# One list for the order of all operations and their engines, in an attention and MoE kernel

## The chip, the cores and the metric

The kernel runs on one core of one Trainium2 chip. The metric is the device time of one launch in microseconds, the median over repeated runs. A core has five instruction queues that the kernel writes: TensorE (PE in the profile, with its weight loads as PEld), VectorE (DVE), ScalarE (ACT), GpSimd (POOL) and SyncE (SP), which issues almost all DMAs. Each queue runs its instructions strictly in the order in which the program gives them; a semaphore makes one wait for another.

## The reference

```python
q_bits = einsum(q, proj) > 0;  k_bits = einsum(k, proj) > 0     # 6 bits: a bucket of each query and key
mask = q_bucket[..., :, None] == k_bucket[..., None, :]
scores = where(mask, q @ k.T / sqrt(64), -1e9)
attn = exp(scores - max); attn = attn / (sum(attn) + 1e-9)
x = (attn @ v), heads side by side                                # 4 batches, 8 heads, 768 x 64 -> 3072 x 512
out = ((x @ w_a) * (x @ w_b)) @ w_out                             # 512 -> 1536 -> 512
```

q, k, v and proj come as float32. The three weight matrices come as float64, 18.9 MB together, and are made into 32-bit floats on the chip.

## The kernel before, in words

**Tiling.** The 3072 tokens are cut into 14 chunks, `CHUNKS`: the first four hold 128 tokens of batch 0, the other ten 256 tokens. Attention is done in units of one head and 128 queries (`qtile`): scores of 128 queries against 768 keys (L1215, with the mask folded in as 12 more rows of the product), the row maximum (L1235, tile `mx`), its scale and bias (`affine`, L1243 and L1247), the exponential (L1256, tile `e`), a turn of the result, and the product with v. The eight units of chunk 0 are turned on TensorE in 32 bits (`turned`, tiles `et` and `at`, copied out by L639); all later ones are split into two 16-bit halves (`by_dma`: a cast by L639 and a subtraction by L642, tile `a`) and turned by a DMA. `su_end` divides by the sum (tile `x`, L1335) and turns x to `xT`. `moe` multiplies a chunk by the weights: first products `ab` (L1442 in 32 bits for chunks 0 and 1, L1450 in 16 bits for the rest), their elementwise product `g` (L1471, L1479), and second products `o` (L1515).

**The start.** k, q and v of batch 0 are loaded in head pairs. `split` scales each into a high and a low half: a gram product on TensorE (L675) bounds the magnitude, VectorE reads it (L662) and makes a power of two (`powers`, L625 and L628); then come the high half (`high`, tile `kt` or `qt`), the low half (L748), turns by TensorE and their copies (L639, tiles `trk`, `trq`), and the bits. v is bounded likewise, and `parts` makes its halves `vh` and `vl` (L1051). The weights come in 18 pieces of two loads each (`to_f32`): ScalarE and one of ScalarE and GpSimd work on the raw words (L955; L945 or L947), and VectorE merges them (L963, tile `wz`). Only three staging slots exist, so a load waits until the merge of three pieces earlier is done, and all that stands behind it on SyncE waits too. Each group of weights has a gram product as well (L981). Beside chunks 0 and 1 the weights are split into 16-bit halves (`halved`, L906).

**What sets the order.** Nothing is issued where it is written. The body only calls `op(engine, duration, function, key, reads, writes, ...)`, which records 3727 operations with their dependencies; `Plan.issue` then issues them. In the kernel before it runs a small event model of the engines, with durations written beside each operation: whenever an engine is free, the ready operation with the lowest number in `PLACES` (one number for each operation, lines 62 to 255) goes next. Where an operation could run on several engines, `ENGINES` gives the one, or the engine that is free first takes it. The model holds VectorE back while GpSimd is busy (`PORT_WAIT`) for operations marked `sbuf`, and counts buffers so that no tile is asked for before one is free. The order in which the model issues is the order of the queues on the chip; the model's times go nowhere else.

The small projection is loaded in two pieces through ScalarE's queue, though the model counts them on SyncE (L579). Two operations, for the identity in 16 bits, issue nothing (one ahead of L586, one in `bounds`); the copy itself stands inside another operation (L740, L861).

Of the kernel before, what the change touches and what calls it, by code (L numbers as in the profile page):

```python
# [61 lines left out]
PLACES = (  # L62
# [234 lines left out]
    3481: "DVE", 3489: "DVE", 3497: "DVE", 3505: "ACT", 3514: "ACT", 3522: "DVE", 3538: "DVE", 3547: "DVE",  # L297
    3568: "ACT", 3576: "ACT", 3584: "ACT", 3592: "DVE", 3601: "ACT", 3634: "DVE", 3635: "DVE", 3725: "DVE",
}

def free(b, **durs):
# [27 lines left out]
HOP = 0.2  # L331
# [35 lines left out]
class Plan:  # L367
# [32 lines left out]
    def issue(self):  # L400
# [4 lines left out]
        for o in ops:  # L405
            o.succs, o.npred, o.ready = [], len(o.preds), 0.0
# [1212 lines left out]
```

## Time and profile before

| what | before |
|---|---|
| median of 3 runs | 903.46 us (902.1 to 903.72) |
| profiled execution, first to last instruction | 900.4 us |
| median less that span | 3.06 us |
| TensorE busy | 871.8 us, 97% |
| VectorE, ScalarE, GpSimd busy | 624.4, 573.4, 450.9 us |
| DMA | 145.31 MB, mean 161 GB/s |

The page of the profile gives only the span for the profiled execution, so its own time is the span and the 3.06 us by which the median is longer. TensorE is busy for nearly the whole span; where it is not, and where it runs at a lower clock, is told by the views by stretch of time.

### The profile page before, as it was taken

The numbers are of one execution on the slowest core, as the hardware profiler recorded it, in microseconds if no ns is written. First come the engines' busy times: TensorE is split into PE (matmuls) and PEld (weight loads), VectorE is DVE, ScalarE is ACT, GpSimd is POOL, SyncE is SP. The second block draws the span as 40 slices with busy tenths as digits, with TensorE's granted clock in tenths as the row PEclk, the third lists the DMA queues.
The fourth block names the chain that finished last, engine by engine and source line by source line (L and its number), as shares of the span: only waits on it lengthen the run. The fifth ranks groups of instructions, "written<-read, shape, count | busy, mean of one in ns | idle before, by whom it ended". The sixth has DMA issues, their size and how long they took to land.

```text
span 900.4 us, 24310 instructions
## 1 busy us (share of the span) xinstructions
PE 871.8 (97%) x9761; PEld 673.8 (75%) x9761; DVE 624.4 (69%) x1446; ACT 573.4 (64%) x1125; POOL 450.9 (50%) x377
## 2 busy tenths in 40 slices
PE   5798999999999999999999999999999999999998
PEld 4677788786877777777777777777777777777775
DVE  6889878897778666777776686777778576633211
ACT  5986565677776878666766675667676466654222
POOL 1255456555735665554455556635556457544111
PEclk9699999999999999999999999999999999999999
DMA  9898667599998999998976788698986757755100
GB/s 331 262 319 232 124 112 158 124 179 220 190 230 148 170 163 161 177 209 169 176 161 128 149 175 169 115 214 170 179 183 148 124 136 130 147 95 100 32 24 24
DMA packets 430433, 145.31 MB, mean 161 GB/s; under 512 B 404080, under 2 KB 422640, under 8 KB 430320
## 3 DMA queue, kind: packets, MB, share of 16 engines
q1 hardware_dynamic: 430160, 143.76, 76.8%
q8 instruction: 76, 1.25, 0.6%
q14 instruction: 37, 0.30, 0.1%
q10 hardware_dynamic: 160, 0.00, 0.0%
HBM read 37.82 MB, written 6.29 MB: 49 GB/s over the span
## 4 chain that ended last, share of the span: by engine, by line
PE 85%; DVE 9%; DMA 2%; issue 2%; ACT 1%; POOL 0%; SPq 0%; DVEq 0%; ACTq 0%; POOLq 0%
PE ab L1450 37%; PE o L1515 20%; PE s L1215 12%; PE av L1284 10%; PE ab L1442 4%; DVE mx L1235 2%; DVE wz L963 1%; PE kt L766 1%; DMA wz<-in_moe_w_out_dram 1%; DVE wz L906 1%; DMA wz<-in_moe_w_b_dram 1%; DMA wz<-in_moe_w_a_dram 1%; DMA pj<-in_proj_dram 0%; PE qb L787 0%; DVE g L1479 0%
## 5 line engine op out<-in xcount | busy, mean ns | idle before, releaser
L642 POOL TENSOR_TENSOR a<-e,a 128x768 f16<-128x768 f32 x184 | 309.4, 1686 | 199.3 <-DVE a L639 87.9
L1450 PE MATMUL ab<-xT,wz 128*128 128x256 f16 (+1 forms) x3456 | 377.5, 264 | 1.4 <-DVE g L1479 1.0
L1450 PEld LDWEIGHTS <-wz 128*128 128x128 f16 x3456 | 310.9, 98 | 52.5 <-issue 3.5
L1256 ACT ACTIVATE e<-s,bias,sc 128x768 f32<-128x768 f32 x192 | 189.8, 989 | 107.4 <-DVE bias L1247 84.5
L1235 DVE TENSOR_REDUCE mx<-s 128x1 f32<-128x768 f32 x192 | 182.7, 953 | 64.1 <-PE s L1215 59.0
L1515 PE MATMUL o<-wz,g 128*128 128x512 f16 (+1 forms) x840 | 215.6, 392 | 0.1
L1495 POOL TENSOR_TENSOR g<-g,g 128x256 f16<-128x256 f32 x132 | 95.8, 726 | 170.8 <-ACT g L1490 164.3
L1215 PE MATMUL s<-trk,trq 76*128 76x384 f16 (+1 forms) x768 | 157.6, 330 | 3.8 <-ACT e L1256 2.5
L1479 DVE SCALAR_TENSOR_TENSOR g<-ab,ab,a 128x256 f32<-128x256 f32 x132 | 63.4, 480 | 105.6 <-ACT a L1471 88.0
L1284 PEld LDWEIGHTS <-at 128*128 128x128 f16 x3312 | 116.9, 98 | 16.2 <-issue 1.7
L1515 PEld LDWEIGHTS <-g 128*128 128x128 f16 x792 | 73.8, 98 | 68.8
L1471 ACT ACTIVATE a<-ab,ab 128x256 f32<-128x256 f32 x132 | 62.2, 471 | 96.2 <-PE ab L1450 79.8
L1284 PE MATMUL av<-vh,at 128*128 128x64 f16 x2208 | 121.6, 193 | 0.7 <-DMA at<-a 0.7
L1215 PEld LDWEIGHTS <-trq 76*128 76x128 f16 (+1 forms) x768 | 70.7, 99 | 45.7 <-issue 9.5
L639 ACT CAST a<-e 128x768 f16<-128x768 f32 x105 | 87.0, 829 | 3.4 <-DMA at<-a 1.4
L1490 ACT CAST g<-g 128x256 f16<-128x256 f32 x132 | 53.0, 401 | 51.3 <-DVE g L1479 41.1
L1284 PE MATMUL av<-vl,at 128*128 128x64 f16 x1104 | 62.3, 193 | 0.0
L639 DVE CAST a<-e 128x768 f16<-128x768 f32 x71 | 42.2, 596 | 14.6 <-ACT e L1256 13.7
L1442 PE MATMUL ab<-xT,wz 128*128 128x128 f32 x384 | 48.1, 278 | 1.3 <-DVE xT L639 0.8
L1442 PEld LDWEIGHTS ab<-xT,wz 128*128 128x128 f32 x384 | 45.5, 192 | 4.6 <-DVE xT L639 1.5
L1247 DVE TENSOR_SCALAR bias<-mx,sc 128x1 f32<-128x1 f32 x180 | 38.6, 214 | 6.3
L1243 DVE TENSOR_SCALAR sc<-mx,cq 128x1 f32<-128x1 f32 x180 | 38.1, 212 | 4.8
(170 smaller groups left out, 775.4 us busy)
## 6 DMA issues: line engine op xcount, KB each, us to landing
rk<-in_k_dram SPq DMA_DIRECT2D x16, 384.0 KB, 4.2
rq<-in_q_dram SPq DMA_DIRECT2D x24, 256.0 KB, 3.5
wz<-in_moe_w_a_dram SPq DMA_DIRECT2D x12, 512.0 KB, 5.7
wz<-in_moe_w_b_dram SPq DMA_DIRECT2D x12, 512.0 KB, 5.3
wz<-in_moe_w_out_dram SPq DMA_DIRECT2D x12, 512.0 KB, 5.7
out_dram<-osb SPq DMA_DIRECT2D x24, 256.0 KB, 2.5
vr<-in_v_dram SPq DMA_DIRECT2D x12, 384.0 KB, 4.7
at<-a SPq DMA_TRANSPOSE x184, 3.5
```

Of the source, the lines that this page charges most:

```text
L639: {"ACT": nc.scalar.copy, "DVE": nc.vector.tensor_copy, "POOL": nc.gpsimd.tensor_copy}[e](out=out, in_=x)
L642: (nc.gpsimd if e == "POOL" else nc.vector).tensor_tensor(out=out, in0=x, in1=y, op=ALU.subtract)
L1215: nc.tensor.matmul(ps.t[:, jj, :HALF], lhsT=trq.t[rows, i, (2 * j + h) * nt + t], rhs=tr.t[rows, i, k0 : k0 + NT // 2].rearrange("p n s -> ...
L1235: lambda: nc.vector.tensor_reduce(out=mx.t[:, col], in_=halves(ps.t), axis=AX.XY, op=ALU.max, negate=True),
L1256: lambda: nc.scalar.activation(flat2(e.t), halves(ps.t), AF.Exp, bias=bias.t[:, col], scale=sc.t[:, col], accum_out=sm.t[:, u : u + 1],),
L1284: nc.tensor.matmul(av.t[:, u, :], lhsT=at.t[:, a + kt, :], rhs=w.t[:, h, kt, :], start=i == 0, stop=i == 3 * NT - 1,)
L1442: nc.tensor.matmul(pl.t[:, m, to], lhsT=wt32(m, cc, f), rhs=xt.t[:, cc * nt // NC, cc * nt % NC : cc * nt % NC + nt, :], start=cc == 0, st ...
L1450: nc.tensor.matmul(pl.t[:, m, to], lhsT=wt(m, wi, cc, f), rhs=xt.t[:, cc * nt // NC, xi, cc * nt % NC : cc * nt % NC + nt, :], start=i == ...
L1471: lambda a=a, pl=pl, gr=gr, sc_of=sc_of: nc.scalar.activation(a.t, pl.t[:, 0, :CH], AF.Copy, scale=sc_of(gr)),
L1479: lambda a=a, g32=g32, pl=pl, gr=gr, sc_of=sc_of: nc.vector.scalar_tensor_tensor(out=g32.t, in0=pl.t[:, 1, :CH], scalar=sc_of(gr + 1), in1 ...
L1495: lambda g=g, g32=g32, g_of=g_of: nc.gpsimd.tensor_tensor(out=g_of(g[1]), in0=g32.t, in1=g_of(g[0]), op=ALU.subtract),
L1515: nc.tensor.matmul(po[u].t.rearrange("p a b -> p (a b)"), lhsT=x()[:, us], rhs=w, start=f == 0 and i == 0, stop=f == NF - 1 and i == len(t ...
```

## The change

`PLACES`, `ENGINES` and the event model in `Plan.issue` go. In their place stand `ORDER`, one list of the 3725 operations that are left, and `ENGINE_OF`, the engine of each operation that has a choice. `issue` walks through the list, asserts that every operation comes after those it depends on and that buffers suffice, and issues it. The two operations that issue nothing go, and what they stood for is stated as reads and writes of the operations that copy the identity. The two loads of the projection are counted on ScalarE's queue, through which they went already. No instruction is added or taken away.

```diff
-PLACES = (
-    372, 36, 26, 591, 571, 25, 386, 254, 1614, 66, 385, 210, 155, 399, 576, 261, 194, 687, 615, 294, 3076, 750, 536,
...
+ORDER = (
+    2, 1, 75, 11, 76, 4, 3, 77, 5, 78, 79, 80, 81, 0, 12, 13, 14, 15, 6, 282, 281, 9, 10, 84, 27, 16, 82, 17, 83, 18,
...
-ENGINES = {
-    17: "DVE", 20: "ACT", 27: "ACT", 33: "DVE", 36: "DVE", 43: "ACT", 49: "DVE", 52: "DVE", 53: "ACT DVE",
...
+ENGINE_OF = {
+    "ACT": (
+        19, 20, 35, 36, 42, 58, 64, 67, 74, 83, 84, 90, 105, 107, 119, 128, 138, 140, 149, 157, 159, 166, 168, 176, 178,
...
     def issue(self):
-        ops = self.ops
-        for o, place in zip(ops, PLACES):
-            o.key = place
-            o.eng = ENGINES.get(o.seq, o.eng)
...
+        engine = {n: e for e, ns in ENGINE_OF.items() for n in ns}
+        issued, live = set(), {}
+        for n in ORDER:
+            o = self.ops[n]
+            assert o.preds <= issued, n
+            issued.add(n)
...
+            if isinstance(o.dur, dict):
+                o.fn(engine[n])
+            else:
+                o.fn()
...
-            "SP", DMA_ISSUE, lambda h=h: nc.scalar.dma_start(out=pj[D * h : D * h + D, :], in_=proj),
+            "ACT", DMA_ISSUE, lambda h=h: nc.scalar.dma_start(out=pj[D * h : D * h + D, :], in_=proj),
...
-    op("DVE", 0.2, lambda: None, -85, r=["csb"], w=["identh"])
...
-            high, key, r=[*toks, ai], w=[(pt[0], "hi")], sbuf=True,
+            high, key, r=[*toks, ai] + ["csb"] * len(first), w=[(pt[0], "hi"), *first], sbuf=True,
```

Set side by side, queue by queue, the two orders differ as follows (an operation may be several instructions).

- TensorE: 1056 operations in both. The first 382 are the same set in another order; from the 383rd on, a second product of chunk 4, both queues are the same to the end.
- VectorE 1047 to 1061 operations (without the two that issue nothing), ScalarE 866 to 857 (without its two loads), GpSimd 361 to 356. The last 660, 595, 256 and, on SyncE, 245 operations are the same in both.
- 105 of the operations with a choice change engine, all in the part that differs. The largest group is 14 subtractions of `by_dma` (L642, 128x768) that go from GpSimd to VectorE.
- SyncE's first loads are rq, rk and the identity, where they were rk, rq and the identity. Then weights come ahead of v: the four loads of v stand at the 16th, 22nd, 23rd and 26th place, where they stood 7th, 8th, 9th and 11th with the projection's two counted.
- TensorE's first operation is the gram of q; it was the bound of the projection, which now stands 5th.

## Rows read from the trace of the kernel before

**Rows 1.** Page of the profile, its head.

```profile
span 900.4 us, 24310 instructions
```

**Rows 2.** Stretches: length, busy us (and count) of each engine, granted clock, DMA share, GB/s.

```profile
...
0.00:76.51 76.51, 56.60 (x569) 47.97 (x569) 63.26 (x149) 60.34 (x86) 25.41 (x32) 0.87 0.93 293
76.51:190.00 113.49, 112.23 (x1266) 91.06 (x1267) 97.43 (x195) 70.83 (x124) 61.56 (x46) 1.00 0.66 147
190.00:282.81 92.81, 90.57 (x1245) 70.89 (x1242) 72.58 (x187) 68.05 (x140) 52.64 (x44) 1.00 1.05 202
282.81:900.40 617.59, 612.40 (x6692) 463.91 (x6688) 391.12 (x918) 374.20 (x777) 311.29 (x256) 1.00 0.74 142
```

**Rows 3.** Stretches, the same view, one of ten us early on.

```profile
...
38.00:48.00 10.00, 8.37 (x54) 0.50 1.01 301
```

**Rows 4.** Timeline of TensorE: start, us, instruction, count [idle before <-releaser].

```profile
...
6.01 0.16 PE L613 MATMUL ps_pj<-st_pj,onesr 128*128 128x1 bf16 x1 [6.01 <-ACT pjx L653]
...
6.63 0.63 PE L675 MATMUL gram_q<-rq 128*128 128x128 bf16 x4
...
76.51 5.62 PE L1442 MATMUL ab<-xT,wz 128*128 128x128 f32 x48 [0.81 <-DVE xT L639]
```

**Rows 5.** Timeline of TensorE, where the two orders join.

```profile
...
282.81 1.46 PE L1515 MATMUL o<-wz,g 128*128 128x512 f16 x6
```

**Rows 6.** Timeline of SyncE's queue at the start, same columns.

```profile
...
0.74 0.45 SPq L1017 DMA_DIRECT2D rk<-in_k_dram  x1
1.24 0.46 SPq L1144 DMA_DIRECT2D rq<-in_q_dram  x1
```

**Rows 7.** Timeline of VectorE, same columns, at the start and around the first MoE product.

```profile
...
6.21 0.16 DVE L625 TENSOR_SCALAR po_t_pj<-ps_pj 128x1 f32<-128x1 int32 x1 [5.07 <-PE ps_pj L613]
...
73.74 0.68 DVE L1335 TENSOR_TENSOR x<-av,r 128x512 f32<-128x512 f32 x1
...
75.77 0.68 DVE L639 COPY xT<-px 128x512 f32<-128x512 f32 x1
```

**Rows 8.** VectorE by line and form, 0 to 140 us: count | busy us, mean ns | idle before.

```profile
...
L963 DVE SCALAR_TENSOR_TENSOR wz<-wz 128x1024 int32<-128x1024 int32 x18 | 24.4, 1368 | 2.7 <-ACT wz L945 1.4 <-POOL wz L947 1.2
L1235 DVE TENSOR_REDUCE mx<-s 128x1 f32<-128x768 f32 x25 | 23.8, 950 | 4.4 <-PE s L1215 3.4 <-PE ps_k L613 0.8
...
L748 DVE SCALAR_TENSOR_TENSOR qt<-rq,ai_q,qt 128x512 f16<-128x512 f32 x5 | 4.2, 835 | 0.1
...
L1051 DVE SCALAR_TENSOR_TENSOR vl<-v,v_ai,vh 128x768 f16<-128x768 f32 x4 | 4.1, 1013 | 0.0
...
L1247 DVE TENSOR_SCALAR bias<-mx,sc 128x1 f32<-128x1 f32 x15 | 3.2, 214 | 0.5
...
L639 DVE COPY trk<-kt 128x1536 f16<-128x1536 f16 x3 | 2.8, 948 | 0.0
...
L639 DVE COPY at<-et 128x384 f32<-128x384 f32 x3 | 1.6, 543 | 0.0
...
L662 DVE TENSOR_REDUCE wst<-gram_w 128x1 bf16<-128x128 f32 x6 | 1.7, 287 | 0.3 <-PE gram_w L981 0.3
...
L628 DVE SCALAR_TENSOR_TENSOR ai_k<-pw,po_t_k 128x2 int32<-128x2 f32 x4 | 0.9, 221 | 0.1
...
L648 DVE TENSOR_SCALAR qt<-rq,ai_q 128x512 f16<-128x512 f32 x1 | 0.5, 478 | 0.0
```

**Rows 9.** One tile, wz, 0 to 100 us: ns min/median/max, first and last start.

```profile
...
L963 DVE SCALAR_TENSOR_TENSOR wz<-wz x18: 1214/1226/2614, 17.9 to 90.8; 128x1024 int32<-128x1024 int32 x18
```

**Rows 10.** TensorE by line and form, 0 to 140 us.

```profile
...
L981 PE MATMUL gram_w<-wz 128*128 128x128 bf16 x96 | 7.3, 233 | 0.1
```

**Rows 11.** Waits of VectorE, 76.51 to 190 us: total us, times, longest.

```profile
...
DVE mx L1235 <- PE s L1215: 5.6, 9, 1.1
```

**Rows 12.** Line 642 on both engines, 0 to 283 us: ns min/median/max.

```profile
...
L642 POOL TENSOR_TENSOR a<-e,a x50: 1638/1646/2676, 69.8 to 281.1; 128x768 f16<-128x768 f32 x50
...
L642 DVE TENSOR_TENSOR x<-x,x x2: 693/804/914, 156.2 to 194.1; 128x512 f16<-128x512 f32 x2
```

More of the change, by code (lines that the diff above doesn't have):

```diff
@@ L1 @@
-import heapq
 from contextlib import ExitStack
@@ L59 @@
 M_LAG, E_LEAD, O_LAG = 5.65, 308.72, 3.89
-PLACES = (
[192 rows of a table removed]
-)
-ENGINES = {
-    17: "DVE", 20: "ACT", 27: "ACT", 33: "DVE", 36: "DVE", 43: "ACT", 49: "DVE", 52: "DVE", 53: "ACT DVE",
-    59: "DVE", 69: "POOL", 81: "ACT", 84: "ACT", 85: "POOL", 91: "ACT", 106: "ACT", 108: "ACT", 117: "POOL",
-    120: "ACT", 122: "ACT", 126: "POOL", 129: "ACT", 131: "ACT", 136: "DVE", 150: "ACT", 155: "POOL", 158: "ACT",
-    160: "DVE", 164: "DVE", 167: "DVE", 169: "ACT", 174: "POOL", 177: "ACT", 179: "ACT", 183: "POOL", 188: "ACT",
-    194: "DVE", 200: "ACT", 203: "ACT", 212: "DVE", 214: "DVE", 220: "POOL", 222: "ACT POOL", 231: "POOL",
-    237: "POOL", 239: "ACT DVE", 246: "DVE", 248: "ACT DVE", 263: "DVE", 265: "DVE POOL", 271: "POOL", 273: "POOL",
-    281: "ACT", 284: "ACT", 289: "ACT", 312: "ACT", 324: "ACT", 329: "ACT", 338: "ACT", 343: "POOL", 352: "POOL",
-    357: "POOL", 364: "POOL", 369: "POOL", 378: "ACT", 383: "ACT", 397: "POOL", 450: "ACT", 508: "ACT", 510: "DVE",
-    512: "ACT", 518: "ACT", 522: "ACT", 524: "ACT", 526: "DVE", 530: "ACT", 534: "ACT", 536: "ACT", 538: "ACT",
-    542: "ACT", 549: "DVE", 552: "DVE", 563: "DVE", 569: "POOL", 571: "ACT", 578: "DVE", 580: "DVE", 586: "DVE",
-    588: "ACT", 597: "ACT", 605: "ACT POOL", 614: "POOL", 622: "ACT", 630: "DVE", 695: "DVE", 702: "ACT",
-    705: "ACT POOL", 714: "DVE", 716: "ACT DVE", 724: "DVE POOL", 733: "ACT DVE", 741: "POOL", 748: "DVE",
-    750: "DVE POOL", 756: "DVE", 758: "ACT", 767: "ACT", 773: "DVE", 775: "POOL", 784: "DVE", 848: "ACT",
-    858: "ACT POOL", 869: "DVE POOL", 875: "DVE", 877: "DVE POOL", 883: "DVE", 885: "DVE POOL", 891: "DVE",
-    893: "ACT DVE", 900: "DVE", 902: "ACT", 910: "ACT DVE", 918: "ACT DVE", 924: "DVE", 934: "DVE", 935: "POOL",
-    942: "DVE", 945: "ACT POOL", 956: "ACT", 962: "DVE", 964: "ACT", 970: "POOL", 972: "DVE POOL", 978: "DVE",
-    980: "ACT", 987: "DVE", 995: "DVE", 997: "DVE POOL", 1003: "DVE", 1005: "DVE POOL", 1011: "DVE", 1013: "POOL",
-    1021: "ACT", 1110: "ACT", 1118: "ACT", 1121: "DVE", 1134: "ACT", 1157: "ACT", 1163: "DVE", 1169: "ACT",
-    1175: "DVE", 1185: "ACT", 1193: "ACT", 1209: "DVE", 1218: "DVE", 1226: "ACT", 1234: "ACT", 1242: "ACT",
-    1252: "POOL", 1261: "DVE", 1271: "ACT", 1274: "ACT", 1284: "ACT", 1287: "ACT", 1314: "ACT", 1322: "DVE",
-    1331: "ACT", 1339: "DVE", 1355: "DVE", 1365: "DVE", 1453: "DVE", 1455: "ACT", 1461: "ACT", 1464: "DVE",
-    1491: "ACT", 1508: "ACT", 1524: "DVE", 1532: "ACT", 1541: "ACT", 1548: "ACT", 1562: "DVE", 1570: "ACT",
-    1578: "DVE", 1603: "ACT", 1619: "ACT", 1628: "ACT", 1629: "DVE", 1719: "DVE", 1725: "ACT", 1728: "ACT",
-    1739: "ACT", 1755: "ACT", 1763: "DVE", 1772: "DVE", 1780: "ACT", 1788: "DVE", 1796: "DVE", 1806: "POOL",
-    1826: "DVE", 1834: "DVE", 1842: "DVE", 1850: "ACT", 1867: "ACT", 1883: "ACT", 1893: "DVE", 1981: "ACT",
-    1992: "ACT", 2005: "DVE", 2015: "DVE", 2018: "DVE", 2040: "ACT", 2046: "ACT", 2056: "ACT", 2072: "ACT",
-    2089: "DVE", 2097: "DVE", 2105: "ACT", 2113: "ACT", 2122: "DVE", 2123: "DVE", 2142: "ACT", 2145: "ACT",
-    2155: "ACT", 2158: "ACT", 2169: "ACT", 2177: "DVE", 2185: "ACT", 2193: "DVE", 2210: "DVE", 2226: "ACT",
-    2236: "POOL", 2324: "ACT", 2326: "DVE", 2332: "ACT", 2346: "ACT", 2354: "DVE", 2370: "DVE", 2379: "ACT",
-    2387: "DVE", 2395: "ACT", 2412: "DVE", 2413: "POOL", 2419: "ACT", 2422: "ACT", 2433: "ACT", 2441: "DVE",
-    2449: "DVE", 2457: "ACT", 2466: "DVE", 2474: "ACT", 2482: "ACT", 2490: "ACT", 2500: "POOL", 2588: "ACT",
-    2590: "ACT", 2596: "DVE", 2599: "ACT", 2626: "ACT", 2634: "DVE", 2659: "DVE", 2667: "ACT", 2676: "ACT",
-    2677: "DVE", 2686: "DVE", 2697: "DVE", 2713: "ACT", 2721: "DVE", 2738: "ACT", 2754: "ACT", 2763: "DVE",
-    2764: "POOL", 2852: "DVE", 2854: "DVE", 2860: "DVE", 2863: "ACT", 2873: "DVE", 2876: "ACT", 2886: "ACT",
-    2889: "DVE", 2899: "DVE", 2911: "ACT", 2917: "ACT", 2935: "ACT", 2943: "DVE", 2951: "ACT", 2960: "DVE",
-    2968: "DVE", 2976: "DVE", 2984: "DVE", 2993: "DVE", 2994: "POOL", 3000: "ACT", 3003: "ACT", 3013: "DVE",
-    3016: "ACT", 3026: "DVE", 3029: "DVE", 3040: "ACT", 3048: "ACT", 3056: "DVE", 3064: "ACT", 3073: "DVE",
-    3081: "DVE", 3089: "ACT", 3097: "ACT", 3106: "DVE", 3195: "DVE", 3197: "DVE", 3203: "ACT", 3206: "ACT",
-    3225: "ACT", 3233: "ACT", 3241: "DVE", 3283: "ACT", 3290: "DVE", 3293: "ACT", 3312: "DVE", 3320: "ACT",
-    3345: "DVE", 3353: "ACT", 3361: "ACT", 3370: "ACT", 3371: "DVE", 3459: "DVE", 3461: "DVE", 3467: "ACT",
-    3481: "DVE", 3489: "DVE", 3497: "DVE", 3505: "ACT", 3514: "ACT", 3522: "DVE", 3538: "DVE", 3547: "DVE",
-    3568: "ACT", 3576: "ACT", 3584: "ACT", 3592: "DVE", 3601: "ACT", 3634: "DVE", 3635: "DVE", 3725: "DVE",
@@ L299 @@
+ORDER = (
[187 rows of a table added]
+)
+ENGINE_OF = {
+    "ACT": (
[11 rows of a table added]
+    ),
+    "DVE": (
[18 rows of a table added]
+    ),
+    "POOL": (
[12 rows of a table added]
+    ),
 }
@@ L350, in __init__ @@
         self.shape, self.dtype, self.name = shape, dtype, name
-        self.real, self.left, self.free_at = None, 0, 0.0
+        self.real, self.left, self.held = None, 0, False
     @property
@@ L400, in issue @@
     def issue(self):
-        ops = self.ops
-        for o, place in zip(ops, PLACES):
-            o.key = place
-            o.eng = ENGINES.get(o.seq, o.eng)
-        for o in ops:
-            o.succs, o.npred, o.ready = [], len(o.preds), 0.0
-        for o in ops:
-            for p in o.preds:
-                ops[p].succs.append(o)
-        free = {e: 0.0 for e in ("PE", "ACT", "DVE", "POOL", "SP")}
-        ready = {e: [] for e in free}
-        for o in ops:
-            if not o.npred:
-                for e in o.eng.split():
-                    ready[e].append(o)
@@ L416, in issue @@
-        live = {}
-        dma_free = 0.0
-        held = set()
-        port = 0.0
-        done = 0
-        now = 0.0
-        events = [0.0]
-        releases = []
-        def can(o):
-            need = {}
-            for b in o.bufs:
-                if b not in held:
-                    for k, _ in b.limits:
-                        need[k] = need.get(k, 0) + 1
-            return all(live.get(k, 0) + need.get(k, 0) <= n for b in o.bufs for k, n in b.limits)
-        while done < len(ops):
-            now = heapq.heappop(events)
-            while events and events[0] <= now:
-                heapq.heappop(events)
-            while releases and releases[0][0] <= now:
-                _, k = heapq.heappop(releases)[0:2]
-                for x in self.tags[k]:
-                    live[x] -= 1
-            for e in free:
-                if free[e] > now:
-                    continue
-                if e == "POOL" and port > now:
-                    continue
-                best = None
-                shut = e == "DVE" and free["POOL"] > now + PORT_WAIT
-                for o in ready[e]:
-                    if shut and o.sbuf:
-                        continue
-                    if o.ready <= now and (best is None or (o.key, o.seq) < (best.key, best.seq)) and can(o):
-                        best = o
-                if best is None:
-                    continue
-                o = best
-                for x in o.eng.split():
-                    ready[x].remove(o)
-                for b in o.bufs:
-                    if b not in held:
-                        held.add(b)
-                        for k, _ in b.limits:
-                            live[k] = live.get(k, 0) + 1
-                dur = o.dur
-                if isinstance(dur, dict):
-                    o.fn(e)
-                    dur = dur[e]
-                else:
-                    o.fn()
-                end = now + dur
-                if e == "DVE" and o.sbuf:
-                    end = max(now, free["POOL"]) + dur
-                    port = end
-                free[e] = end
-                if o.svc:
-                    dma_free = max(dma_free, end) + o.svc
-                    fin = dma_free + DMA_TAIL
-                else:
-                    fin = end + (PE_TAIL if e == "PE" else 0.0)
-                for b in o.bufs:
-                    b.left -= 1
-                    b.free_at = max(b.free_at, fin + HOP)
-                    if not b.left:
-                        if b.ring is not None:
-                            b.ring.append(b.real)
-                        if not hasattr(self, "tags"):
-                            self.tags = []
-                        self.tags.append([k for k, _ in b.limits])
-                        heapq.heappush(releases, (b.free_at, len(self.tags) - 1))
-                        heapq.heappush(events, b.free_at)
-                for s in o.succs:
-                    s.ready = max(s.ready, end if s.eng == e and not o.svc else fin + HOP)
-                    s.npred -= 1
-                    if not s.npred:
-                        for x in s.eng.split():
-                            ready[x].append(s)
-                        heapq.heappush(events, max(now, s.ready))
-                heapq.heappush(events, end)
-                done += 1
-            if not events and done < len(ops):
-                raise RuntimeError("no operation can start")
@@ L501, in issue @@
-        return now
+        engine = {n: e for e, ns in ENGINE_OF.items() for n in ns}
[4 more added lines that the diff above has]
+            issued.add(n)
+            for b in o.bufs:
+                if not b.held:
+                    b.held = True
+                    for k, limit in b.limits:
+                        live[k] = live.get(k, 0) + 1
+                        assert live[k] <= limit, (n, k)
+            if isinstance(o.dur, dict):
+                o.fn(engine[n])
+            else:
+                o.fn()
+            for b in o.bufs:
+                b.left -= 1
+                if not b.left:
+                    for k, _ in b.limits:
+                        live[k] -= 1
+                    if b.ring is not None:
+                        b.ring.append(b.real)
@@ L504, in attention_moe @@
+        assert len(issued) == len(self.ops)
 @with_exitstack
@@ L740, in high @@
                 nc.vector.tensor_copy(out=identh, in_=ident)
+        first = ["identh"] * (x == "0_0" and which == "k")
         op(
             "ACT DVE", {"ACT": 0.3 + 0.83e-3 * size, "DVE": 0.24 + 0.54e-3 * size},
-            high, key, r=[*toks, ai], w=[(pt[0], "hi")], sbuf=True,
+            high, key, r=[*toks, ai] + ["csb"] * len(first), w=[(pt[0], "hi"), *first], sbuf=True,
         )
@@ L848, in bounds @@
     def bounds(key, tag):
-        op("DVE", 0.2, lambda: None, key, r=["csb"], w=["identb"])
         mx = buf("b_mx", [P, 2], F32, "b_mx", 1, cp)
@@ L865, in both @@
                 )
-        op("DVE", 0.2, both, key, r=[*((wst, g) for g in range(NG)), wo_ai], w=[wm], sbuf=True)
+        op("DVE", 0.2, both, key, r=["csb", *((wst, g) for g in range(NG)), wo_ai], w=[wm, "identb"], sbuf=True)
         ps = psum("ps_bounds", tag)
```

417 rows, old and new, of tables (ENGINE_OF, ORDER, PLACES) are left out of this document.

## The prediction

> **What bounds the kernel now.** Read the head of the page first: the profiled execution spans 900.4 us [rows 1], 3.06 us less than the median of 903.46 us. I take these 3.06 us, which lie outside the first and last instruction, as fixed, and make the sum against 900.4.
>
> Then the view by stretches, TensorE's column first [rows 2]. Length less busy time is its idle time: 19.91 us up to 76.51, 1.26 up to 190, 2.24 up to 282.81, 5.19 over the 617.59 us after that. So TensorE bounds the kernel everywhere but in the first 76.51 us, and nearly all that a new order can win is there. 76.51 is the start of the first MoE product (the gate, below), 282.81 the start of the second product with which the two orders join [rows 4, 5]. From that instruction on every queue holds the same instructions in the same order. I carry those 617.59 us over unchanged; their 5.19 us of idle time are the most that could come or go by another phase between the engines.
>
> Before the gate a second thing costs time: the clock. Between 38 and 48 us the granted clock is 0.50, its lower level of 1.2 GHz, while TensorE is busy for 8.37 of 10 us [rows 3]; over the whole stretch the mean is 0.87 [rows 2].
>
> Next, who holds the gate. The product waits for a copy on VectorE, tile xT [rows 4]. That copy starts at 75.77, the division that makes x at 73.74 [rows 7]. VectorE is busy for 63.26 of these 76.51 us, more than TensorE (56.60), ScalarE (60.34) or GpSimd (25.41) [rows 2], and its first real work came only at 6.21, after 5.07 us of waiting [rows 7]. So before the gate VectorE is the bound, and the right question to the new list is how much work it puts on VectorE ahead of x.
>
> **The change, part by part.** *Work on VectorE ahead of x.* I compared the two VectorE queues up to the operation that makes x. 22 operations leave that part of the queue: 3 merges of weights at 1.226 us (the median [rows 9]; 3.68), 2 low halves of v at 1.013 (2.03), 2 copies of turned keys at 0.948 (1.90), 1 row maximum (0.95), 2 copies of turned exponentials and a cast, all at 0.543 (1.63), 2 scale and bias pairs at twice 0.214 (0.86), 3 powers at twice 0.221 (1.33, at most), 3 readings of a gram at 0.287 (0.86), and 3 one-column products at 0.214 (0.64) [rows 8]. Sum 13.88. 14 enter it: a copy of turned keys (0.95), 3 high halves of q at 0.478 (1.43), 3 copies at 0.543 (1.63), 4 scale and bias pairs (1.71), a gram (0.29), a power (0.44) and a low half of q at 0.835 (0.84) [rows 8]. Sum 7.29. The net is 6.59 us less; I take 6.0, since the powers were priced at most and instructions overlap a little at their ends (18 merges of 1.368 make 24.62, but 24.4 busy [rows 8]). The copy to xT goes from VectorE to ScalarE; I count it at nothing, since it leaves a queue that held it until 75.77 and joins one that is 60.34 of 76.51 busy. On ScalarE 19 operations leave and 9 enter ahead of the last copy of turned exponentials that x needs, so that queue does not become the later one.
>
> *The start.* TensorE's queue began with the bound of the projection, which waited 6.01 us for ScalarE and the projection's load; the grams of k and q stood behind it and then ran without a wait [rows 4]. Now the gram of q is first, and its load is issued first, at the place of 0.74 instead of 1.24 [rows 6]. When that load lands is not in a row. If only at 6.0, nothing is won; it can't land before its issue ends at 1.20, so the gain is below 4.8. I take 1.0, close to the lower end, because the q load itself is moved by only 0.5. The two loads of the projection went through ScalarE's queue already; counting them there moves nothing by itself.
>
> So the gate comes 7.0 us earlier, at about 69.5.
>
> *Work of TensorE that moves behind the gate.* Six operations leave its queue ahead of the gate, two of them grams of weights, and two small ones enter. Six grams took 7.3 us [rows 10], 1.22 each; with the small ones I take 2.0 us net. They must be done later, where TensorE is full, so 7.0 less 2.0, that is 5.0, is won at the gate. A faster clock before the gate is not counted: VectorE sets the gate, and TensorE would only wait longer.
>
> *Between the gate and the join.* VectorE gets 14 operations more over the whole part. 14 subtractions of 128x768 come from GpSimd, where one takes 1.646 (median). VectorE's price for this size is not shown; the same line on 128x512 took 0.693 and 0.914 [rows 12], by size 1.04 to 1.37. Eight of them stand early enough to fall before 190, 8.3 to 11.0 us. With the 6.0 us that moved behind the gate VectorE has at most 97.43 + 6.0 + 9.7 = 113.1 us to do in 113.49 + 7.0 = 120.5. It fits with 7.4 us to spare, where the kernel before had 16.06 [rows 2]. Later merges of weights stand deeper in its queue, 5 to 9 us of work later for those of the fifth and sixth group, and TensorE's products that need them stand later too. I therefore leave TensorE's idle time here at the 1.26 + 2.24 us of before; the bounds are 3.5 us less and, if VectorE falls behind, some 9 more.
>
> *SyncE and its loads.* v moves behind ten and more loads of weights. Each pair of those waits for a merge three pieces earlier, so v now waits for VectorE too. I count it at nothing: the merges it waits for come earlier: the first seven stand 1 to 7 us of VectorE's work nearer its start, by the same prices. If that cover is gone, the products of TensorE that read v hold the gate (second rival).
>
> Sum: 7.0 - 2.0 = 5.0 us less, 895.4 us of span, **898.5 us** in the median's terms.
>
> **The rivals.** *Held instructions go as well: 894.* A merge takes 1.226 us in the median and 2.614 at most [rows 9], as if it were held now and then; 18 merges were busy for 24.4 us [rows 8] where 18 medians make 22.1, so 2.3 us were lost in this line alone. The list moves work off GpSimd. If VectorE sets TensorE's pace up to 190 and such losses (I take twice 2.3, for the other lines with them) go, 4.6 us more are won: 893.9. Against it: GpSimd was busy for only 25.41 us before the gate.
>
> *The gate is not VectorE's: about 903.7.* If a late load of v, or the turn from engine to engine for each unit, holds the gate at 76.51, then the 2.0 us moved behind it cost and nothing is won: 905.5. If half of the 7.0 comes through, 903.46 - 3.5 + 2.0 = 902.0. I take the middle, 903.7. For it: the load of v behind weights. Against it: VectorE's 63.26 busy us.
>
> *VectorE falls behind after the gate: 907.* The place is the stretch from the gate to 190. Of the 16.06 us in which VectorE was not busy there, at least 5.6 were waits for scores of TensorE [rows 11], which shrink when VectorE is late; the rest are gaps and answers of other engines, which don't. If all 16.06 recur, VectorE is 16.06 - 7.4 = 8.7 us late at 190 and TensorE with it: 898.5 + 8.7 = 907.2. It decides between loss and gain when more than 12.4 us recur. Against it are the 5.6 us, and that TensorE need not wait for each late result.
>
> A rule bears on this rival: the page "SBUF — State Buffer" of the Trainium skill, section "SBUF: two separate sides", says that VectorE and GpSimd share one pair of ports as an exclusive lock, which a VectorE operation with two inputs in SBUF needs against a GpSimd operation that reads SBUF; the loser is held for the whole instruction. The subtractions that move are of that kind. The trace can't decide it with two cases, of 0.693 and 0.914 us for one size [rows 12]. By this rule the eight could each be held for one GpSimd subtraction; at 1.646 that is 13.2 us, and this rival's time would be 911.7.
>
> *The list changes the order on paper only: 903.5.* If the queues on the chip came out in the order of before, nothing would move.
>
> **How the numbers follow.** Chances: the forecast 0.50, with a range of its own of 895.5 to 901.5; held instructions go too 0.17; gate not VectorE's 0.17; VectorE falls behind 0.12; paper only 0.04. The range from 891.5 to 904.5 holds the first two whole and most of the third, and leaves out the fourth. Differences under 0.2% (901.65 to 905.27) can't be told from no change here. Faster: 0.50 + 0.17 + 0.05 of the third case, 0.72. Same: 0.11 of the third and 0.04 for paper only, 0.15. Slower: 0.12 and the last 0.01 of the third, 0.13.
>
> **What would show it.** In the trace after: TensorE's first matmul is a gram of q, before 6 us; L1335 runs near 67 and the first L1442 near 69.5, with VectorE busy for some 57 us before it; TensorE idle for 14 to 16 us up to the gate; a second product that followed at 282.81 now at about 277.8, and 617.6 us behind it as before. The forecast is wrong if the gate moves by less than 3 us, if TensorE is idle for over 8 us between gate and join, or if the part after the join is not within 2 us of 617.6.

## The result, and the profile after

| | before | after |
|---|---|---|
| median | 903.59 us (4 runs) | 891.65 us (4 runs, 891.48 to 892.21) |
| profiled execution, first to last instruction | 900.4 us | 890.4 us |
| start to gate (first MoE product) | 76.51 us | 64.61 us |
| gate to join (first instruction from which both orders agree) | 206.30 us | 208.17 us |
| join to end | 617.59 us | 617.62 us |

The ratio of the medians is 0.9867, with a 95% interval of 0.9852 to 0.9881: 11.9 us less where I forecast 5.0. In the two profiles 11.9 us go ahead of the gate, 1.9 come back between gate and join, and behind the join nothing moves.

Between the medians' 11.9 and the spans' 10.0 lie 1.9 us. Most of it is my use of the profile of before: 13 later executions of that kernel have a median span of 902.1 us and 1.80 to 1.88 us outside it. So the profiled 900.4 was a quick one, and my 3.06 us "outside" were 1.85 and that luck. Where the gate lies in a median execution of the kernel before is not on record; the 76.51 us are those of the quick one.

The view by stretches of after, which answers to [rows 2] (start and end, length, then busy time and count of TensorE, its weight loads, VectorE, ScalarE, GpSimd, then granted clock, share of the DMA engines, GB/s). The first line ends at x, the second at the gate:

```profile
0.00:61.87 61.87, 49.34 (x509) 42.52 (x510) 54.87 (x134) 46.99 (x70) 21.41 (x25) 1.00 0.91 301
0.00:64.61 64.61, 52.08 (x538) 44.79 (x539) 57.61 (x141) 48.89 (x74) 22.82 (x28) 1.00 0.92 305
64.61:178.00 113.39, 111.60 (x1279) 90.33 (x1278) 104.57 (x219) 84.42 (x143) 60.80 (x46) 1.00 0.91 180
178.00:272.78 94.78, 92.91 (x1262) 73.35 (x1260) 77.59 (x183) 58.63 (x126) 43.89 (x42) 1.00 0.95 180
272.78:890.40 617.62, 612.41 (x6688) 463.94 (x6685) 391.28 (x921) 373.96 (x777) 310.48 (x256) 1.00 0.75 143
```

The same view of before up to its x, and from VectorE's first real work up to it; in the second fence the latter stretch of after:

```profile
0.00:73.74 73.74, 55.60 (x563) 47.47 (x563) 60.52 (x142) 58.20 (x84) 24.53 (x30) 0.86 0.92 297
6.21:73.74 67.53, 55.40 (x562) 47.16 (x560) 60.19 (x136) 56.41 (x80) 23.15 (x24) 0.85 0.93 307
```

```profile
4.70:61.87 57.17, 48.73 (x505) 42.07 (x505) 54.53 (x128) 45.50 (x68) 20.04 (x19) 1.00 0.94 312
```

x comes 11.87 us earlier. VectorE has 5.65 us less to do ahead of it (60.52 less 54.87). It starts 1.51 us earlier (4.70 for 6.21). And between its start and x it is idle for 2.6 us (57.17 less 54.53) where it was for 7.3. Less work, an earlier start, fewer waits: 5.65 + 1.51 + 4.7 = 11.9.

The waits themselves, of VectorE from 0 to x: total us, times, longest. Before:

```profile
DVE po_t_pj L625 <- PE ps_pj L613: 5.1, 1, 5.1
DVE wz L963 <- ACT wz L945: 1.4, 1, 1.4
DVE mx L1235 <- PE s L1215: 1.3, 2, 0.9
DVE wz L963 <- POOL wz L947: 1.2, 2, 0.7
DVE mx L1235 <- PE ps_k L613: 0.8, 1, 0.8
```

After:

```profile
DVE st_q L583 <- PE gram_q L596: 3.6, 1, 3.6
DVE onev L513 <- PEq L1519: 0.8, 1, 0.8
DVE po_t_k L546 <- PE ps_k L534: 0.3, 1, 0.3
DVE po_t_k L546 <- PE ps_pj L534: 0.3, 1, 0.3
DVE po_t_q L546 <- PE ps_q L534: 0.3, 1, 0.3
DVE wz L884 <- issue: 0.3, 1, 0.3
```

No merge (L884, which was L963) waits for a third and no row maximum (L1156, which was L1235) for scores any more. At the gate TensorE no longer stands still: two units of scores fill the time that the copy to xT takes (TensorE's timeline of after, as [rows 4]):

```profile
62.86 0.60 PE L1297 MATMUL px<-ident,x 128*128 128x128 f32 x4
63.30 1.47 PE L1136 MATMUL s<-trk,trq 76*128 76x384 f16 x8
64.61 0.61 PE L1363 MATMUL ab<-xT,wz 128*128 128x128 f32 x4
```

### The profile page after: what moved, and what is told of

It reads as the page before. It is cut to its first block, busy times and chain, and to the rows that moved or that the text cites. A ratio compares the mean times of both kernels' runs of the same rounds, so it can differ in the third digit from the quotient of the medians.

```text
span 890.4 us, 24299 instructions
## 1 busy us (share of the span) xinstructions
PE 869.0 (98%) x9761; PEld 672.4 (76%) x9761; DVE 631.1 (71%) x1461; ACT 565.9 (64%) x1116; POOL 438.0 (49%) x371
## 4 chain that ended last, share of the span: by engine, by line
PE 70%; DVE 3%; issue 1%; ACT 0%; DVEq 0%; ACTq 0%
PE ab L1371 35%; PE o L1436 17%; PE s L1136 10%; PE av L1205 8%; DVE vh L569 0%; DVE g L1400 0%; PE qb L709 0%; DVE mx L1156 0%; PE kb L709 0%; DVE hp L736 0%; DVE hp L739 0%; DVE ai_q L549 0%; DVE osb L569 0%; DVE kt L670 0%; PE ps_cx L768 0%
## 5 line engine op out<-in xcount | busy, mean ns | idle before, releaser
L563 POOL TENSOR_TENSOR a<-e,a 128x768 f16<-128x768 f32 x170 | 286.2, 1687 | 186.7 <-ACT a L560 84.0
L1156 DVE TENSOR_REDUCE mx<-s 128x1 f32<-128x768 f32 x192 | 182.6, 953 | 53.2 <-PE s L1136 49.1
L1136 PE MATMUL s<-trk,trq 76*128 76x384 f16 (+1 forms) x768 | 155.0, 327 | 2.4 <-ACT e L1177 1.8
L560 ACT CAST a<-e 128x768 f16<-128x768 f32 x102 | 84.5, 829 | 3.0 <-DMA at<-a 1.2
L560 DVE CAST a<-e 128x768 f16<-128x768 f32 x68 | 39.4, 580 | 14.0 <-ACT e L1177 14.0
```

The costliest lines, as they stand in the source:

```text
L560: {"ACT": nc.scalar.copy, "DVE": nc.vector.tensor_copy, "POOL": nc.gpsimd.tensor_copy}[e](out=out, in_=x)
L563: (nc.gpsimd if e == "POOL" else nc.vector).tensor_tensor(out=out, in0=x, in1=y, op=ALU.subtract)
L1136: nc.tensor.matmul(ps.t[:, jj, :HALF], lhsT=trq.t[rows, i, (2 * j + h) * nt + t], rhs=tr.t[rows, i, k0 : k0 + NT // 2].rearrange("p n s -> ...
L1156: lambda: nc.vector.tensor_reduce(out=mx.t[:, col], in_=halves(ps.t), axis=AX.XY, op=ALU.max, negate=True),
```

## The experiments

The changed kernel, run again in the last set, had its gate at 64.61 again and a median of 892.82. That run's profile is the second one of the changed kernel. So gates can be compared closely, while its medians in two sets differ by 1.2 us. Where both are told, the gate tells what happened ahead of it; what a run lost behind it is told by the time from gate to join.

**One part of the list on the kernel before.**

```diff
 start:    SyncE rk rq -> rq rk; TensorE ps_pj gram_k gram_q ps_k ps_q -> gram_q ps_q gram_k ps_k ps_pj
 order:    ORDER of after, every engine as before (105 operations differ)
 engines:  ORDER of before, ENGINE_OF of after
 v late:   before, with v's 4 loads, 4 grams and their readings, its power and 8 halves at the new places
```

Start:

> The kernel before with one part of the new list alone: the load of q is issued ahead of that of k, TensorE begins with the gram of q, then its bound, the gram and bound of k, and only then the bound of the projection; VectorE's first ten operations follow in that order. Theory A (VectorE, busy from its first operation to x, sets the gate, so an earlier start is handed on whole): first VectorE operation near 4.7 us, first MoE product near 75.0, 902.0 us. Rival (the start is lost again in the next waits for loads): gate at 76.5, 903.5 us.

Order:

> The new order of all operations, but every operation on the engine that it had before (105 operations differ, some 25 of them ahead of x). Theory A (what counts is how much of VectorE's queue stands ahead of x, and its start): VectorE has some 1.4 us less to do ahead of x than in the changed kernel, gate at 63 to 65 us, 890 to 892 us. Rival B (the engines chosen for the thirds of the weights and the scale and bias pairs took away VectorE's waits of 4.7 us): the waits come back, gate near 69, 896 us or more.

Engines:

> The order of before, but every operation on the engine that the new list gives it. Theory A: VectorE's work ahead of x is 1.4 us more than before and its start the same, so 903 to 905 us. Rival B (engine choices took the waits away): the waits of 4.7 us on ScalarE, GpSimd and TensorE shrink, gate near 72, 899 us.

V late:

> The kernel before, its engines and its order, with one part of the new list: the four loads of v, their grams, powers and halves (22 operations) stand in each queue at the place that the new list gives them, weights' loads ahead of them. Theory C (that v stands late is the core of the gain): weights land up to 4.4 us earlier, two low halves (2.0 us) leave the part of VectorE's queue ahead of x, its waits for thirds shrink: gate at 71 to 73, 898 to 900 us. Rival S (the parts of the list are fitted to each other and none wins by itself, as with the order and the engines alone): 903 us or more.

| kernel | gate | gate to join | median |
|---|---|---|---|
| before | 76.51 | 206.30 | 903.35 to 904.16 in the sets |
| start | 76.15 | 206.88 | 902.29, ratio 0.998 (0.997 to 0.999) |
| order | 81.39 | 232.59 | 934.19, ratio 1.0337 (1.0321 to 1.0353) |
| engines | 83.95 | 218.67 | 919.62, ratio 1.0181 (1.0161 to 1.0200) |
| v late | 86.66 | 213.32 | 921.95, ratio 1.0213 (1.0190 to 1.0235) |
| after | 64.61 | 208.17 | 891.65, ratio 0.9867 |

The start gives the time of theory A, but not in its way: VectorE starts at 4.59 us, and the gate moved by 0.36 us, not by 1.5. Between its start and x VectorE is idle for 8.8 us, where it was for 7.3, so most of the earlier start was lost in waits. Why the median is 1.7 us below that of before in its set is not shown. Of the others, "v late" is as rival S had it, and worse; "engines" lies beyond every theory of mine, and "order" 12 us beyond the gate of rival B. "Order" has less work on VectorE up to x than after has (53.26 us busy for 54.87), and its x is 15 us later, at 76.99. A count of work is not enough: the waits decide. And the gate is less than half of what "order" loses to after: from gate to join it takes 24.4 us more, in which TensorE is idle for 21.0 us, where it is for 3.7 in after. Waits of VectorE up to x in "order":

```profile
DVE mx L1167 <- PE s L1147: 4.4, 3, 3.2
DVE st_q L594 <- PE gram_q L607: 3.5, 1, 3.5
DVE at L571 <- PE et L1123: 3.2, 1, 3.2
DVE trk L571 <- PE kt L699: 2.3, 1, 2.3
DVE wz L895 <- ACT wz L887: 1.9, 1, 1.9
```

**Parts of after taken back.**

```diff
 loads:   SyncE rq rk ident w w rk w w rk rk ... v -> rq rk ident rk v v v w v w ...
 thirds:  "POOL": 283, 311, 323, 328, 337, 382, 391 -> "ACT"; "ACT": 342, 363, 368, 396 -> "POOL"
 pairs:   "DVE": 125, 154, 173, 182 -> "POOL"
```

Loads:

> The changed kernel with the four loads of v where the kernel before issues them, ahead of the weights (the other queues keep the new order). Theory A with my step on the loads (their order is worth nothing, since loads land well ahead of use): 891.7 us, gate at 64.6. Rival C (the 16 DMA engines are full for the first 30 us, and weights ahead of v are what lets the merges run without a wait): 1.57 MB more stand ahead of the first weights, VectorE waits 2 to 4 us at its first merge, gate 2 to 4 us later, 894 to 896 us.

Thirds:

> The changed kernel with the eleven thirds of weights that changed engine back on the engine that they had before (7 of them from GpSimd to ScalarE, 4 from ScalarE to GpSimd; five of the former ahead of x). Rival B (thirds on ScalarE made the merges wait): ScalarE has some 5 us more ahead of x, merges wait 2 us or more in all, 894 us or more. Theory A: ScalarE is busy for 47.0 of the 61.9 us ahead of x and takes it: 891.7 us, within 0.7.

Pairs:

> The changed kernel with the scale and bias pairs of four units of the first scores on GpSimd, as before the change, in place of VectorE (4 times 0.43 us less on VectorE ahead of x; on GpSimd such a pair takes 0.8 us). Theory A on counts: gate up to 1.7 us earlier, 890.0 us. Rival B (a pair on GpSimd stands behind thirds of weights of 1.6 us each that wait for loads, and the exponential waits for it): gate 1 us or more later, 892.7 us or more.

Loads: gate 69.37, 897.38 us. Thirds: gate 73.46, 903.22 us. Pairs: gate 66.41, 894.25 us. The rivals, C and B, have the nearer time in each, but the waits are not where C and, in "thirds", B had put them, at the merges: merges wait 1.2 us for thirds in "loads" and 1.2 in "thirds". In "pairs" the way is B's in part: the exponential on ScalarE waits 4.4 us for GpSimd's bias (0.8 in after), but the one long wait, 3.5 us, is for a pair that stands behind two copies (tile `hp`, 2.3 us), not behind thirds. The old place of v's loads costs 4.8 us at the gate; TensorE's wait there:

```profile
PE gram_k L607 <- DMA rk<-in_k_dram: 5.7, 1, 5.7
```

The load of a pair of keys stands behind v, its gram comes late, and VectorE, which reads this gram next, stands still for 3.0 us.

The engines of the thirds are worth 8.9 us at the gate in the new order, and the trace shows the way of the longest wait from engine to engine. ScalarE, TensorE and VectorE of "thirds" (start, length, what ran; in brackets the idle time before it and its cause):

```profile
40.78 1.10 ACT L877 ACTIVATE wz<-wz 128x1024 int32<-128x1024 uint8 x1 [2.25 <-DMA wz<-in_moe_w_a_dram]
41.78 1.42 ACT L571 COPY trk<-kt 128x1536 f16<-128x1536 f16 x1
```

```profile
43.26 1.44 PE L1147 MATMUL s<-trk,trq 76*128 76x384 f16 x4 [5.04 <-ACT trk L571]
```

```profile
44.73 0.96 DVE L1167 TENSOR_REDUCE mx<-s 128x1 f32<-128x768 f32 x1 [4.90 <-PE s L1147]
```

A third waits for its load on ScalarE; the copy of turned keys behind it waits with it; the scores wait for the copy, VectorE's maximum for the scores. VectorE's wait carries TensorE's name, its root is a load at the head of ScalarE's queue. In after GpSimd waits for such loads instead (tile wz up to x, the part on who waited for its loads and writers: us, times):

```profile
  POOL wz L868: 24.0, 6
  ACT wz L876: 0.3, 1
```

**Are the thirds enough?**

```diff
 thirds alone:      ORDER and engines of before, the eleven thirds on their new engines
 order and thirds:  ORDER of after, the thirds on their new engines, the other 94 as before
```

Thirds alone:

> The kernel before with the eleven thirds of weights on the engines that the new list gives them (7 from ScalarE to GpSimd, 4 the other way) and nothing else. Theory F (a third that waits for its load on ScalarE holds what stands behind it there; the choice of engine for the thirds is by itself the gain): ScalarE's 2.7 us of waits for weights go, gate 2 to 4 us earlier, 899 to 902 us. Rival S (the choice pays only in the order made for it: in the old one GpSimd's copies for the turned q and k stand behind the thirds): 905 us or more.

Order and thirds:

> The new order with the thirds on their new engines and the other 94 operations on those of before. With all 105 on the old engines it took 934.2 us, with the thirds alone on the old ones 903.2. Theory F (the thirds are most of what the engines are worth): 895 to 905 us. Rival S (each group of choices is fitted to the order, and their losses add or come in one another's place): 915 us or more.

Thirds alone: gate 80.00, 906.82 us, ratio 1.0033 (1.0015 to 1.0051). Order and thirds: gate 76.54, 929.01 us; its gate is 11.9 us behind that of after, and from gate to join it takes 230.74 us, 22.6 more. Theory F falls, and the times are rival S's. The reason that S gave for the first, GpSimd's copies behind the thirds, is not what VectorE's waits show: in the order of before a merge waits 2.7 us for a third on GpSimd, and merges still wait 2.1 us for ScalarE.

**VectorE as the bound, and the clock.**

```diff
 more:  + 15 tensor_reduce(out=pjx[:, :1], in_=ident) on VectorE behind operation 33
 less:  VectorE's vh vl vh vl of the pairs 2 and 3 moved behind x
 warm:  + 14 matmul(ps.t[:, 1, :256], lhsT=onesr, rhs=onesr[:, 0:1] broadcast) ahead of the gram of q
```

More:

> The changed kernel with 15 idle maxima over a 128x128 tile added to VectorE's queue behind its 13th operation, near 14 us; such readings of 128x128 start 0.20 us apart when they follow each other, so 3.0 us of work that nothing needs. Theory A (VectorE, without waits, sets the gate): gate 3.0 us later, 894.7 us. Rival T (TensorE and its clock set it, VectorE has slack): gate under 1.5 us later, at most 893.2 us.

Less:

> The changed kernel with the two high and low halves of v that x doesn't read (4 operations of VectorE, 52.0 to 55.5 us, some 3.0 us of its time) moved behind x. Theory A with VectorE as the only bound: gate 3.0 us earlier, 888.7 us. Rival T: TensorE runs without a gap from 53.8 us to the gate and ends the last product that x reads at 61.19, 0.7 us ahead of x, so the gate can come 0.7 us earlier at most: 891.0 us or no change.

Warm:

> The changed kernel with 14 products of 128x128 by 256 columns on TensorE ahead of its first gram, in the 4.0 us in which it waits for the first load; they read a constant and nothing reads them. In the changed kernel TensorE's products take the lower clock's time until 26 to 28 us. Rival E (that clock costs time): the products go over to the higher clock's time earlier, gate 1.5 to 3 us earlier, 889 to 890 us. Theory A: VectorE holds the gate, TensorE only waits longer: 891.7 us, within 0.5, whatever the clock does.

More: gate 67.02, 894.25 us. The 15 readings took 4.8 us, not 3.0, yet the gate moved by 2.41 only. I read that as no slack: VectorE's busy time up to the gate rose by only 2.27 (59.88 for 57.61), since others got shorter, and its idle time hardly changed (7.14 us for 7.00). The 11 merges take 13.8 us for 14.8 there, the four writes of q's bits 0.7 for 1.7. Gate and busy time move together, as theory A says.

Less: gate 66.26, 899.0 us, worse than either theory. Only 1.7 us of that lie ahead of the gate; from gate to join it takes 213.25 us for 208.17, TensorE being idle for 2.3 us more and busy for 2.8 us more, with a granted clock of 0.89 from 75 to 100 us. VectorE came to the next merge earlier and waited there:

```profile
DVE wz L895 <- ACT wz L877: 3.3, 1, 3.3
```

That merge starts at 55.41 us, in after at 55.52: the four operations had filled the time in which ScalarE made that third. To take work off the bounding engine won nothing while its next input was not there.

Warm: gate 64.96, 893.25 us, no gain over 891.65 and 892.82. The grams show that the clock did change (TensorE's timeline of "warm", then of after):

```profile
1.20 3.12 PE L606 MATMUL gram_q<-onesr 128*128 128x256 bf16 x14 [1.20 <-DVE onesr L518]
...
5.20 0.52 PE L612 MATMUL gram_k<-rk 128*128 128x128 bf16 x6
10.81 0.85 PE L612 MATMUL gram_k<-rk 128*128 128x128 bf16 x6
```

```profile
5.11 0.82 PE L596 MATMUL gram_k<-rk 128*128 128x128 bf16 x6
10.92 0.85 PE L596 MATMUL gram_k<-rk 128*128 128x128 bf16 x6
```

With the products ahead a gram near 5 us takes 0.52, without them 0.82; at 10.8 both are slow. The faster TensorE near 5 us did not bring the gate forward: rival E falls for that stretch. For a part of the rest the second profile of the changed kernel speaks: there the gram of k at 13.39 us took 0.52 (0.82 at 13.24 in the first), scores at 26.34 took 0.81 (1.41 at 26.80), TensorE was busy for 50.26 us up to the gate instead of 52.08, and the gate was the same:

```profile
0.00:64.61 64.61, 50.26 (x538) 43.26 (x539) 57.64 (x141) 49.18 (x74) 22.64 (x28) 0.92 0.92 304
```

**Can it be better?**

```diff
 c1:  "DVE": 80, 16 -> "ACT"; VectorE does the power of k and the projection's parts meanwhile
 c2:  gram of the third chunk's q, its reading, power and high half behind x
 c3:  c1, and SyncE rq rk ident w w rk -> rq rk ident rk w w
```

c1, c2, c3, and after beside them:

> The changed kernel with the first two scalings (q 0.49 us, k 0.62 us) on ScalarE, which is busy for 1.1 of the 6 us there; VectorE does the power of k and the projection's parts meanwhile. Theory A (VectorE's work near its start sets the gate, as 3.0 us more of it cost 2.6): gate 1.0 us earlier, 890.7 us. Rival D (the DMA engines are full from 4 to 30 us, so merges wait for weights if VectorE comes to them earlier): gate unchanged, 891.7 us, within 0.5.

> The changed kernel with the gram of the third chunk's q and what VectorE makes of it (0.28, 0.44 and 0.48 us, near 32 to 37 us) moved behind x, on TensorE and VectorE. Theory A: gate 1.0 us earlier, 890.7 us. Rival S (as with the halves of v, the merge that moves up waits for its third): no gain, 891.7 us or more.

> As the run with the first scalings of q and k on ScalarE (gate 0.8 us earlier, VectorE then waited 2.2 us for a gram of k whose load stands behind two loads of weights), and this load of k issued ahead of those two. Theory A: VectorE doesn't wait there, gate at 62 to 63, 890 us. Rival D (the thirds of the weights then come 1 us later, and a merge waits in place of the gram): gate at 63.5 to 65, no gain on the changed kernel measured beside it.

> The changed kernel itself, as the measure for the run beside it: 891.7 us, within 0.7.

c1: gate 63.84, 892.58 us. c2: gate 64.80, 895.36; x came 0.7 us earlier, the gate did not, and from gate to join it takes 211.13 us for 208.17. c3: gate 66.07, 892.07, beside 892.82 for after in the same set: no difference. In c3 VectorE's wait for the gram of k (2.2 us, as in c1) stayed, and another came; its waits up to x:

```profile
DVE st_k L594 <- PE gram_k L607: 2.6, 2, 2.2
DVE po_t_q L557 <- PE ps_q L545: 1.7, 2, 1.4
```

The load that c3 moves was not what this gram waited for. It is the second gram of k, and in TensorE's queue it stands behind the turn of the first keys, which waits for VectorE's low half:

```profile
10.24 1.46 PE L699 MATMUL kt<-identh,kt 128*128 128x128 f16 x12 [1.38 <-DVE kt L681]
11.50 0.85 PE L607 MATMUL gram_k<-rk 128*128 128x128 bf16 x6
```

No variant is shown to be faster than after.

## Why the forecast was too small

| step | forecast | measured |
|---|---|---|
| work on VectorE ahead of x | -6.0 | -5.65 |
| the start | -1.0 | -1.51 |
| waits of VectorE on the way to x | not counted | -4.7 |
| gate | -7.0 | -11.9 |
| work of TensorE behind the gate | +2.0 | +1.7 |
| idle time of TensorE from gate to join | 0 | +0.16 |
| join to end | 0 | +0.03 |

The step that failed is "So the gate comes 7.0 us earlier". It adds the work and the start, and silently carries over the 7.3 us in which VectorE stood idle between its start and x; 4.7 of them went. [Rows 8] had shown 2.7 of them ahead of merges, 1.4 behind ScalarE's thirds and 1.2 behind GpSimd's, and I used that row for the merges' length alone. What the runs put in its place: 4.7 us of waits went, and the waits follow from how order, engines and loads fit each other. The thirds back on ScalarE bring 8.9 us back at the gate, v ahead of the weights 4.8, four pairs on GpSimd 1.8. That is no split of the 4.7, since no part won them by itself on the kernel before; which share is the order's, the engines' or the clock's (below) stays open.

"SyncE and its loads", counted at nothing, failed with it: in the new order the place of v's loads is worth 4.8 us. And of ScalarE I asked only whether its queue would become the later one, not what waits in it for loads.

What held: VectorE as the holder of the gate, in the sense that time added to it delays the gate ("more") and that the gate comes 2.7 us behind x in both kernels; time taken off it brought the gate 0.8 us forward in c1, and not at all in "less" and c2. Its work counted from the queues, within 0.35 us (my plain sum was 6.59, which is 0.9 off); the 2.0 us behind the gate; the idle time between gate and join (3.66 us for 3.50); the part after the join. Of the signs I named, the gram of q came first, at 4.05 us, and the part after the join is within 0.03; x, the gate and the join came 5 us ahead of theirs, and TensorE's idle time up to the gate, 12.53 us, is under the 14 to 16 (14.35 in the second profile, with the same gate).

The clock was left out of the sum. TensorE's work up to the join took 2.8 us less (256.6 for 259.4). I put this down to the low stretch of [rows 3], in which the same scores took 1.44 to 1.49 us for 0.82 in after. "TensorE would only wait longer" is not shown for the kernel before: both waits of its VectorE for scores, 0.33 and 0.94 us, fall on products that ran in that stretch, the longer one here (TensorE, then VectorE):

```profile
46.92 1.44 PE L1215 MATMUL s<-trk,trq 76*128 76x384 f16 x4
```

```profile
48.40 0.96 DVE L1235 TENSOR_REDUCE mx<-s 128x1 f32<-128x768 f32 x1 [0.94 <-PE s L1215]
```

So by these two waits up to 1.3 of the 4.7 us can be the clock's and not the list's. The later executions of the kernel before point the same way: of 50 in four sets, the ten with a mean granted clock of 0.991 or more have a median span of 900.45 us, the 17 with 0.987 or 0.988 one of 902.3. No run takes the two apart; "warm" and the second profile tell only that TensorE's early stretches don't move the gate of the changed kernel.

The rivals. "Held instructions go as well" has the nearest time, but not the cause: merges ahead of x take 1.342 us in the mean after, 1.265 before, and between gate and join nothing was won (208.17 us for 206.30). "The gate is not VectorE's" falls by the gate itself, 11.9 us earlier, and by the run "more". "VectorE falls behind" did not come: it is busy for 104.57 of 113.39 us after the gate, 8.8 to spare where I had 7.4. A subtraction of 128x768 takes 0.95 us on VectorE, less than my 1.04.

On the rule of the Trainium skill on the shared ports ("SBUF — State Buffer", section "SBUF: two separate sides"): one merge of after looks just like it. It starts at 30.23 and takes 2.18 us; GpSimd's third runs from 30.18 for 1.15, and from its end on the merge needs another 1.08. But of the six subtractions of 128x768 on VectorE up to 178 us the median is 0.951 and the longest 1.572, so the 13.2 us that I had worked out from the rule did not come. My 911.7 was also a wrong sum: it left out the 7.4 us that I had to spare, and with them 13.2 us would have given 904.3.

## What to carry to other kernels

A gate's time has three terms on the engine that holds it: its start, its work and its waits; follow each wait to its root before carrying it over unchanged. What waits for a load holds all that stands behind it in its engine's queue, so see what that is in the order at hand: the same eleven thirds on the same engines took 11.6 us off in the new order (891.65 us for 903.22) and added 3 us in the old one. And judge a list as a whole: its order or its engines alone were 16 to 30 us slower than the kernel before, and more than half of that lay behind the gate.

## What the runs showed that I had not expected

The column of the granted clock says 1.00 for the whole profile of after, while a gram of k takes 0.82 to 0.85 us up to 18 us and one of the same six products over v 0.50 at 34.85: the durations show the lower level early on, the column does not. In the second profile it says 1.00 up to 12 us, where the same grams take 0.80 and 0.85, and 0.50 from 16 to 24 us. And 14 products that nothing reads brought the higher level for the grams near 5 us, but at 10.8 it was gone again.
